# First loads in quarters, spread rows by DMA, and due-time ranks that reach into batch 1: a fused attention and MLP kernel

## The chip, the cores and the metric

The kernel runs on one core of a Trainium2 chip. The metric is the device time of one execution in microseconds. Beside the timed runs there is one execution recorded by the hardware profiler; every view quoted here is of such an execution. TensorE (PE in the rows, with PEld for its weight loads) multiplies matrices, VectorE (DVE), ScalarE (ACT) and GpSimd (POOL) do elementwise work, and SyncE (SP) issues most DMAs. Each engine runs its own instructions strictly in order.

## The reference, cut to what matters

```python
kv  = einsum('bhsd,bhse->bhde', k, v)            # 8 batches, 8 heads, 576 tokens, 64 wide
o   = einsum('bhsd,bhde->bhse', q, kv)
o   = o / sqrt(mean(o*o, -1) + 1e-6) * g_norm    # per head
x   = o as [batch, 576, 512]
tok = einsum('ts,bsd->btd', w_tok, alpha1*x + beta1)
u   = x + lam * tok
ch  = relu((alpha2*u + beta2) @ w_ch1) @ w_ch2   # 512 -> 2048 -> 512
out = u + lam * ch
```

All inputs and the output are f32. No softmax is involved, so K and V are multiplied first, into a 64 by 64 matrix for each head.

## The kernel before, in words

**Tiling.** A batch of 576 tokens is four chunks of 128 tokens and a tail of 64; the tails of two batches share a chunk, so that odd batches carry 640 columns through the channel products and even ones 512. For each batch TensorE computes: K times V (L674, tails L684; for batch 0 L610), q times that (L765 and L390; for batch 0 L772), token mixing (L854, tails L876; for batch 0 L906), the transposes of u (L941 in batches 0 and 1, by DMA later), 16 first channel products (ch1: L988 in even batches, L1002 in odd ones) and 16 or 20 groups of four second channel products (ch2: L1024). ScalarE applies ReLU to ch1's results (L979). VectorE normalises: squares on ScalarE (L800), then a sum (L802), a reciprocal (L808), the product with it (L821) and with alpha1, g and lam (L825, giving `rt`, the input of token mixing). GpSimd multiplies by g (L829).

**Startup.** Batch 0 is done in f32. `load_first` (L508) loads the four heads of a half of K and of V with one DMA each: 96 partitions, each with six consecutive tokens of 256 bytes per head (`six`, L463). `kv_first` (L599) multiplies them: six chunks of tokens times four heads, the heads in two column halves of TensorE, into one PSUM bank. `qt_first` (L624) turns q, its tail by four products with a 64 by 64 identity per half of the heads (L646). w_tok is transposed on TensorE (L1159, L1177). The weights w1 come in four loads, are cast by ScalarE and VectorE (L490, L491), and the products with beta2 give ch1's bias (L1255). w2 comes in four loads and is multiplied by lam (L1269) on VectorE or GpSimd. The rows lam, alpha2, e1 (alpha1 times g and lam) and g are needed on all 128 partitions: each is loaded as one row and spread by TensorE, a column of ones times the row (`spread`, L1089; product L1096), then copied from PSUM.

**Order of the work.** All operations go through `Prog.op` (L71) with an engine (or a choice of engines), a cost in us, and what they read and write. `schedule` (L169) is a list scheduler: it keeps a clock for every engine, gives each the first ready operation in order of priority (`pri`; the source order unless said otherwise) and so writes down the static order in which each engine will run. A DMA's end is modelled by one queue: `dma_free = max(dma_free, t + 0.3) + lat`, plus 2.0. Among TensorE's operations, only the first 16 in the order of priority are looked at once ch1 has begun; before that, a product of zeros (`warm`, L1330) fills in where nothing is ready. `hasten` (L105) walks back from targets with due times and gives everything that they depend on, SP's DMAs apart, a priority ahead of all else by the length of its way; `plan` (L122) then reschedules some rounds, computes each operation's latest start, ranks by it, and keeps the round whose modelled end is earliest. The targets were the 16 ch1 products of batch 0, 0.87 us apart (L1332). All else, batch 1's attention and token mixing among it, kept the source order; `merge` (L1296) sets that.

SP's loads are chained in their order (`P.chain`): the first K, V, q halves, w_tok, two loads of w1, batch 1's K and V, w1, batch 1's q, w1, then the four of w2, then batch 2.

Of the kernel before, what the change touches and what calls it, by code (L numbers as in the profile page):

```python
# [17 lines left out]
DM = 512  # L18
# [30 lines left out]
class Prog:  # L49
# [55 lines left out]
    def hasten(self, targets, step):  # L105

        rank, due = {}, {o: step * i for i, o in enumerate(targets)}
# [14 lines left out]
    def plan(self, targets, step, rounds):  # L122
# [3 lines left out]
        ahead = self.hasten(targets, step)  # L126
# [42 lines left out]
    def schedule(self):  # L169
# [226 lines left out]
def bass_transnormer_attn__then__resmlp_affine_kernel(  # L396
# [15 lines left out]
    with ExitStack() as stack:  # L412
# [50 lines left out]
        def six(tile, a):  # L463
            return tile[0:96, a].rearrange("p h c d -> p (h c d)")[:, 0:1536].rearrange(
                "p (h c d) -> p h c d", h=4, c=6)
# [27 lines left out]
        def load_main(tile, key, src, b, hs, eng="SP"):  # L493
# [4 lines left out]
                dma_us=3.6 * (hs.stop - hs.start) / 8)  # L498
# [9 lines left out]
        def load_first(a):  # L508
            for key, src, tile in (("kf", k, kf), ("vf", v, vf)):
                P.op("SP", 0.6, lambda e, src=src, tile=tile: e.dma_start(  # L510
                    six(tile, a).rearrange("p h c d -> p h (c d)"),
                    src[0, HALVES[a], :, :].rearrange("h (p c) d -> p h (c d)", c=6)),
                    w=[(key, a)], dma_us=2.05)

        def load_kv(b, go=()):
            j = (b + 1) % 2
            for tile, tl, src, n in ((kf, kft, k, "kf"), (vf, vft, v, "vf")):
# [3 lines left out]
                    r=go, w=[(n, j)], dma_us=3.6)  # L521
# [77 lines left out]
        def kv_first():  # L599

            def group(a):
                t = P.ptile(1)

                def f(e):
                    ks, vs = six(kf, a), six(vf, a)
                    for c in range(6):
                        for h in range(4):
                            o = t.flat(slice(64 * (h % 2), 64 * (h % 2) + 64))[
                                :, 64 * (h // 2):64 * (h // 2) + 64]
                            m = e.matmul(o, ks[:, h, c, :], vs[:, h, c, :],  # L610
                                         start=(c == 0 and h < 2), stop=(c == 5),
                                         skip_group_check=True)
                    return m
                P.op("PE", 1.7, f, r=[("kf", a), ("vf", a)], w=[t])
                for h in range(2):
# [3 lines left out]
                        t.flat(rows)[:, 0:128].rearrange("p (r e) -> p r e", r=2)),  # L619
                        r=[t, "kvz"], w=[("kv32", a, h)])  # L620
# [3 lines left out]
        def qt_first():  # L624

            def pair(pr):
# [9 lines left out]
                P.op("PE", 1.0, f, r=["ident", ("qf", pr // 2)], w=[t])  # L636
# [3 lines left out]
            def tail(a):  # L640
                t = P.ptile(1)

                def f(e):
                    for pr in range(2):
                        for h in range(2):
                            m = e.matmul(t.flat(slice(64 * h, 64 * h + 64))[  # L646
                                :, 64 * pr:64 * pr + 64], qft[0:64, 4 * a + 2 * pr + h, :],
                                ident[0:64, 0:64], start=True, stop=True)
                    return m
                P.op("PE", 0.4, f, r=["ident", "qft0"], w=[t])  # L650
# [326 lines left out]
        def ch1_groups(b):  # L977
            def relu(t, src, dst, fj, n):
                P.op("ACT", act_us(n) + 0.09, lambda e: e.activation(  # L979
                    dst, src(), ACT.Relu, bias=hb[:, fj:fj + 1]),  # L980
                    r=[t, ("hb", fj // 4)], w=[("ht", fj)])

            def even(fj):
# [9 lines left out]
                first_ch1.append(o)  # L993
                relu(t, lambda: t.flat(), ht[:, fj, 0:512], fj, 512)

            def odd(fj):
# [10 lines left out]
                P.op("PE", 1.1, f, r=[("w1", fj // 4)] + [("a2t", i) for i in range(5)],  # L1007
# [355 lines left out]
```

## Time and profile before

| | |
|---|---|
| median of 3 runs | 373.29 us (373.05 to 374.56) |
| the profiled execution | 372.88 us, its span 371.1 us |
| TensorE busy | 359.2 us, 97% of the span |
| VectorE, ScalarE, GpSimd busy | 197.0, 166.2, 79.9 us |
| DMA | 59.33 MB, mean 160 GB/s |
| granted TensorE clock | 0.999 |

The span runs from the first to the last instruction of the program. Busy time counts an instruction from its start to its modelled end; TensorE's products overlap one another, so a busy TensorE need not be at its peak. A row of the timeline reads: start, length, engine, line of the kernel, operation, out and in, shapes, count, and in brackets how long the engine idled before it and who ended that. In the chain of waits, each piece is a start, a length, and what the end of the program waited for at that time.

### The profile page before, as it was taken

How to read it: one execution, taken by the hardware profiler on the slowest of the kernel's cores; microseconds unless marked ns; L12 is line 12 of the kernel's file. 1: busy time of each engine (PE TensorE's matmuls, PEld its weight loads, DVE VectorE, ACT ScalarE, POOL GpSimd, SP SyncE). 2: the span in 40 equal slices, each digit the busy share in tenths (PEclk: the TensorE clock that was granted, in tenths of full speed). 3: DMA queues.
4: the chain of work that ended last, by engine and by line, in shares of the span. 5: the costliest groups of instructions: out<-in, count | busy, mean ns of one | idle time of the engine just before them, and what ended most of it. 6: DMA issues, size and time to landing. Idle time of an engine off the chain costs nothing.

```text
span 371.1 us, 6911 instructions
## 1 busy us (share of the span) xinstructions
PE 359.2 (97%) x3074; PEld 208.9 (56%) x2838; DVE 197.0 (53%) x300; ACT 166.2 (45%) x268; POOL 79.9 (22%) x69
## 2 busy tenths in 40 slices
PE   7999999999999999999999999999999999999995
PEld 3887665466654554457664554457654554457642
DVE  3267598976566467834836166924833175720021
ACT  1466797217862088206670087207730186007500
POOL 4046008520242005300242006200520006100000
PEclk9999999999999999999999999999999999999999
DMA  8999999989969399439923399423503110330021
GB/s 191 252 349 296 327 384 300 265 195 253 282 130 226 110 300 225 54 115 260 245 51 86 127 306 185 76 101 58 113 8 107 58 30 1 66 114 5 2 83 58
DMA packets 92456, 59.33 MB, mean 160 GB/s; under 512 B 59454, under 2 KB 83526, under 8 KB 92298
## 3 DMA queue, kind: packets, MB, share of 16 engines
q1 hardware_dynamic: 92400, 58.88, 63.1%
q8 instruction: 23, 0.38, 0.4%
q14 instruction: 7, 0.06, 0.0%
q10 hardware_dynamic: 26, 0.01, 0.0%
HBM read 38.04 MB, written 9.44 MB: 128 GB/s over the span
## 4 chain that ended last, share of the span: by engine, by line
PE 88%; DMA 4%; DVE 4%; ACT 1%; issue 1%; SPq 1%
PE ps L1024 30%; PE ps L1002 18%; PE ps L988 14%; PE ps L854 8%; PE ps L674 4%; DMA qf<-in_q_dram 4%; PE ps L390 2%; PE ps L765 2%; PE ps L876 1%; PE ps L906 1%; PE ps L941 1%; DVE small L802 1%; DVE rt L825 1%; PE ps L684 1%; SPq L510 1%
## 5 line engine op out<-in xcount | busy, mean ns | idle before, releaser
L1024 PE MATMUL ps<-w,ht 128*128 128x512 bf16 x551 | 126.0, 379 | 2.5 <-issue 1.7
L979 ACT ACTIVATE ht<-ps,hb 128x512 bf16<-128x512 f32 (+1 forms) x128 | 93.4, 742 | 46.0 <-PE ps L1002 38.8
L1024 PEld LDWEIGHTS ps<-w,ht 128*128 128x128 bf16 x576 | 54.5, 98 | 64.1 <-issue 1.2
L829 POOL TENSOR_TENSOR xm<-xm,g_bc 128x512 f32<-128x512 f32 (+1 forms) x36 | 46.4, 1288 | 190.3 <-DVE rt L825 188.4
L1002 PE MATMUL ps<-a2t,w 128*128 128x320 bf16 x512 | 72.0, 299 | 0.5 <-ACT ht L979 0.5
L1002 PEld LDWEIGHTS ps<-a2t,w 128*128 128x128 bf16 x512 | 49.2, 98 | 21.6 <-ACT ht L979 1.3
L988 PE MATMUL ps<-a2t,w 128*128 128x512 bf16 x246 | 57.0, 379 | 0.6 <-issue 0.2
L1033 DVE TENSOR_TENSOR xm<-ps,xm 128x512 f32<-128x512 f32 x32 | 22.1, 689 | 63.6 <-PE ps L1024 63.4
L701 ACT ACTIVATE kvd<-ps 64x128 bf16<-64x128 f32 x28 | 7.6, 272 | 86.0 <-PE ps L684 85.6
L988 PEld LDWEIGHTS ps<-a2t,w 128*128 128x128 bf16 x256 | 23.9, 98 | 26.3
L802 DVE TENSOR_REDUCE small<-sq 128x16 f32<-128x1024 f32 (+3 forms) x27 | 25.3, 936 | 23.6 <-ACT sq L800 23.6
L861 DVE TENSOR_TENSOR xm<-ps,xm 128x1024 f32<-128x1024 f32 x14 | 17.0, 1220 | 21.8 <-PE ps L854 21.8
L854 PE MATMUL ps<-rt,wt 128*128 128x512 bf16 x106 | 27.5, 379 | 0.4 <-DVE rtt L825 0.2
L800 ACT ACTIVATE sq<-ps 128x1024 f32<-128x1024 f32 (+3 forms) x27 | 21.6, 798 | 6.7 <-PE ps L772 3.5
L562 DVE TENSOR_TENSOR qs<-qf,qs 128x2048 bf16<-128x2048 f32 (+1 forms) x10 | 16.4, 1659 | 9.4 <-ACT qs L490 9.3
L706 DVE TENSOR_TENSOR kvd<-ps,kvd 64x128 bf16<-64x128 f32 x28 | 8.1, 289 | 25.0 <-ACT kvd L701 24.4
L765 PEld LDWEIGHTS ps<-kvd,qt 128*128 128x128 bf16 x280 | 17.9, 98 | 4.2
L821 DVE TENSOR_TENSOR xm<-ps,small 128x1024 f32<-128x1024 f32 (+1 forms) x18 | 19.7, 1098 | 0.4
L825 DVE TENSOR_TENSOR rt<-xm,e1g_bc 128x1024 bf16<-128x1024 f32 (+1 forms) x17 | 19.4, 1140 | 0.2
L490 ACT ACTIVATE qs<-qf 128x2048 bf16<-128x2048 f32 (+1 forms) x8 | 12.7, 1588 | 14.9 <-DMA qf<-in_q_dram 12.3
L390 PE MATMUL ps<-kvd,qt 128*128 128x64 bf16 x280 | 19.2, 193 | 0.0
L765 PE MATMUL ps<-kvd,qt 128*128 128x64 bf16 x280 | 19.1, 193 | 0.0
(107 smaller groups left out, 293.0 us busy)
## 6 DMA issues: line engine op xcount, KB each, us to landing
out_dram<-xm SPq DMA_DIRECT2D x32, 256.0 KB, 2.4
kf<-in_k_dram SPq DMA_DIRECT2D x7, 1024.0 KB, 9.5
vf<-in_v_dram SPq DMA_DIRECT2D x7, 1024.0 KB, 7.3
qf<-in_q_dram SPq DMA_DIRECT2D x7, 1024.0 KB, 8.7
stg<-in_moe_w_ch_dram SPq DMA_DIRECT2D x3, 1024.0 KB, 12.3
kf<-in_moe_w_ch_dram SPq DMA_DIRECT2D x2, 1024.0 KB, 14.5
kf<-in_k_dram SPq DMA_DIRECT2D x2, 576.0 KB, 8.4
vf<-in_v_dram SPq DMA_DIRECT2D x2, 576.0 KB, 10.4
```

The lines of the kernel that those rows point to most:

```text
L390: return pe.add_instruction(mybir.InstMatmult(start_tensor_calc=start, stop_tensor_calc=stop, tile_size=(128, 128), tile_position=(0, 0), ...
L765: e.matmul(o, w, kvd[:, h, 0, :], start=True, stop=False)
L800: P.op("ACT", act_us(64 * m), lambda e: e.activation(sqv, raw(), ACT.Square), r=[t], w=[("sq", sqs)])
L802: P.op("DVE", dve_us(64 * m), lambda e: e.tensor_reduce(out=smv, in_=sqv.rearrange("p (h d) -> p h d", h=m), axis=AX.X, op=ALU.add), r=[(" ...
L825: lambda e: e.tensor_tensor(out=r_, in0=x, in1=eb, op=ALU.mult),
L829: P.op("POOL", pool_us(64 * nh), lambda e, xc=xc: e.tensor_tensor(out=xc, in0=xc, in1=g_bc[rows, None, :].to_broadcast([nr, nh, DH]), op=A ...
L854: m = e.matmul(t.ap()[:, i, :], tok_w(b, sc, c), rsrc(b, sc), start=(sc == 0), stop=(sc == 4))
L979: P.op("ACT", act_us(n) + 0.09, lambda e: e.activation(dst, src(), ACT.Relu, bias=hb[:, fj:fj + 1]), r=[t, ("hb", fj // 4)], w=[("ht", fj)])
L988: m = e.matmul(t.flat(), w1[:, dj, 128 * fj:128 * fj + 128], a2t[:, dj, 0:512], start=(dj == 0), stop=(dj == 3))
L1002: m = e.matmul(t.ap()[:, i, 0:320], w1[:, dj, 128 * fj:128 * fj + 128], a2t[:, dj, 320 * i:320 * i + 320], start=(dj == 0), stop=(dj == 3))
L1024: m = e.matmul(t.flat(), ht[:, fj, 128 * c:128 * c + 128], w2[:, fj, :], start=(fj == 0), stop=(fj == 15))
L1033: P.op("DVE", dve_us(512), lambda e: e.tensor_tensor(out=x, in0=t.flat(), in1=x, op=ALU.add), r=[t] + keys, w=keys)
```

## The change

1. The first K and V: four DMAs of two heads take the place of two of four heads, per half. A pair of heads lies on 64 partitions, nine consecutive tokens (2,304 bytes) on each; the other pair on the other 64. `kv_first` multiplies nine chunks of tokens over 64 partitions, the heads alternating between the two halves of the rows, into two PSUM banks. New keys "kfg" and "vfg" stand for the second pair.
2. q's tail is turned by two transposes of two heads each, not by four products.
3. lam and alpha2 are no longer spread by TensorE; a DMA reads the row 128 times into all partitions (`spread_load`). lam's goes behind the last w1 load, alpha2's behind the last w2 load. The row load of alpha2 on ScalarE's queue goes; lam's row stays, for e1.
4. The planner: targets with due times are now ch1 of batch 0 (0.87 us apart), its ReLUs (each 1.5 steps behind its product), ch2 of batch 0 (from 16 us on, 0.87 apart) and the first ch1 product of batch 1 (36 us). All that these depend on, batch 1's attention and token mixing included, is ranked by due time, the targets too. Eight rounds are planned, not six.
5. The costs that the planner assumes for DMAs rise: q 4.2 us (3.6), K and V 3.8 (3.6), a start 0.6 us after issue (0.3); the quarters 1.05.

The diff, cut to its core:

```diff
-    def hasten(self, targets, step):
+    def hasten(self, due):
-        rank, due = {}, {o: step * i for i, o in enumerate(targets)}
+        rank = {}
...
-            if o not in due and o.eng != "SP":
+            if o.eng != "SP":
                 o.pri = -1000.0 - way
...
-        movable = [o for o in ahead if o.eng != "SP" and o not in targets]
+        movable = [o for o in ahead if o.eng != "SP"]
...
-            base = max(o.start - step * n for n, o in enumerate(targets))
-            for n, o in enumerate(targets):
-                late[o] = base + step * n
+            base = max(o.start - d for o, d in due.items())
+            for o, d in due.items():
+                late[o] = base + d
...
-                        dma_free = max(dma_free, t + 0.3) + pick.lat
+                        dma_free = max(dma_free, t + 0.6) + pick.lat
...
+        def nine(tile, a, g):
+            return tile[64 * g:64 * g + 64, a].rearrange("p h c d -> p (h c d)")[
+                :, 0:1152].rearrange("p (h c d) -> p h c d", h=2, c=9)
...
             for key, src, tile in (("kf", k, kf), ("vf", v, vf)):
-                P.op("SP", 0.6, lambda e, src=src, tile=tile: e.dma_start(
-                    six(tile, a).rearrange("p h c d -> p h (c d)"),
-                    src[0, HALVES[a], :, :].rearrange("h (p c) d -> p h (c d)", c=6)),
-                    w=[(key, a)], dma_us=2.05)
+                for g in range(2):
+                    P.op("SP", 0.45, lambda e, src=src, tile=tile, g=g: e.dma_start(
+                        nine(tile, a, g).rearrange("p h c d -> p h (c d)"),
+                        src[0, 4 * a + 2 * g:4 * a + 2 * g + 2].rearrange(
+                            "h (p c) d -> p h (c d)", c=9)),
+                        w=[(key, a)] if g == 0 else [(key + "g", a)], dma_us=1.05)
...
-                    r=go, w=[(n, j)], dma_us=3.6)
+                    r=go, w=[(n, j), (n + "g", j)], dma_us=3.8)
...
+                    for c in range(9):
+                        for h in (0, 2, 1, 3):
+                            g, r = h // 2, slice(64 * (h % 2), 64 * (h % 2) + 64)
+                            m = e.matmul(t.ap(r)[:, g, 0:64], nine(kf, a, g)[:, h % 2, c, :],
+                                         nine(vf, a, g)[:, h % 2, c, :],
+                                         start=(c == 0), stop=(c == 8), skip_group_check=True)
...
+                        h = 4 * a + 2 * pr
+                        m = e.transpose(t.flat()[:, 64 * pr:64 * pr + 64],
+                                        qft[0:64, h:h + 2, :].rearrange("p h d -> p (h d)"),
+                                        ident[0:64, 0:64])
...
+        def spread_load(src, dst, key):
+            P.op("SP", 0.6, lambda e: e.dma_start(dst[:], src[None, :].to_broadcast([128, DM])),
+                 w=[key], dma_us=0.9)
...
-        spread(("lam", "a2"))
...
-        first_ch1 = []
+        due = {}
+
+        def mark(b, ch, i, o):
+            if (b, ch) == (0, 0):
+                due[o] = 0.87 * i
+            elif (b, ch) == (0, 1):
+                due[o] = 16 + 0.87 * i
+            elif (b, ch, i) == (1, 0, 0):
+                due[o] = 36
...
         load_w(3)
+        spread_load(moe_lam, lam_bc, "lam")
...
             load_w(i)
+        spread_load(moe_alpha2, a2_bc, "a2")
...
-        P.plan(first_ch1[:16], 0.87, 6)
+        P.plan(due, 8)
```

More of the change, by code (lines that the diff above doesn't have):

```diff
@@ L644, in f @@
                     for pr in range(2):
[L645 to L648, printed above, removed]
+                        h = 4 * a + 2 * pr
+                        m = e.transpose(t.flat()[:, 64 * pr:64 * pr + 64],
+                                        qft[0:64, h:h + 2, :].rearrange("p h d -> p (h d)"),
+                                        ident[0:64, 0:64])
                     return m
-                P.op("PE", 0.4, f, r=["ident", "qft0"], w=[t])
+                P.op("PE", 0.28, f, r=["ident", "qft0"], w=[t])
                 P.op(act_dve(128), 0, lambda e: copy(
@@ L1026, in f @@
                     return m
[L1027 to L1028 removed]
+                o = P.op("PE", 0.87, f, r=[("w2", n)]
+                         + [("ht", i) for i in range(4 * n, 4 * n + 4)], w=[t])
+                mark(b, 1, 4 * n + c if b == 0 else 4 * c + n, o)
                 if n < 3:
@@ L1086, in load_params @@
                     r=["lamr", "e2r", "rtt0"], w=[("rtt1", i)])
-            spread(("e1", "g"))
-        def spread(names):
-            late = [] if "g" in names else [("wtm", sc) for sc in range(5)]
             for src, row, dst, key in params:
-                if key not in names:
+                if dst is None:
                     continue
```

62 lines of the change are left out of this document (25 added, 37 removed).

## The prediction

> **What bounds the kernel now.** I read the page's first line, then the busy time of each engine in four stretches: up to the first product of data, from there to the first channel product of batch 0, from there to the first channel product of batch 1, and the rest. Columns: stretch, its length, busy time of each engine, granted clock, share of the DMA engines, GB/s.
>
> ```profile
> span 371.1 us, 6911 instructions
> ...
> 0.00:9.00 9.00, 7.14 (x26) 2.75 (x26) 3.38 (x8) 1.49 (x2) 4.28 (x12) 1.00 0.82 187
> 9.00:42.36 33.36, 31.86 (x436) 26.41 (x440) 17.45 (x40) 19.42 (x41) 9.97 (x12) 1.00 1.09 302
> 42.36:86.11 43.75, 43.11 (x404) 24.63 (x371) 37.28 (x56) 25.65 (x48) 15.58 (x9) 1.00 1.03 285
> 86.11:371.10 284.99, 277.05 (x2213) 155.10 (x2004) 138.92 (x198) 119.61 (x179) 50.08 (x36) 1.00 0.52 123
> ```
>
> The reader is to see two things. TensorE (first figure) is busy almost without a break from 9.00 us on, at a clock of 1.00 throughout, so work taken off it can shorten the time. And up to 86.11 us the DMA engines are full as well (1.09, 1.03), after it half empty (0.52). The change acts ahead of 86.11 us; the last stretch I take as unchanged, apart from small shifts of a new plan.
>
> Busy time includes filler: products of zeros (L1330) that run where nothing else is ready. The same view for that line alone:
>
> ```profile
> 9.00:42.36 33.36, 2.07 (x8) 0.81 (x9) 1.00 1.09 302
> ```
>
> So of the 33.36 + 43.75 = 77.11 us between 9.00 and 86.11, TensorE spends 31.86 + 43.11 - 2.07 = 72.90 us on work, 2.07 on filler, and idles for 2.14. Filler and idle, 4.21 us, are all that a better order of this stretch could win; more must come from less work or an earlier start.
>
> Next the chain that ended last (start, length, what), to see what stands on TensorE's path:
>
> ```profile
> 32.69 1.05 PE ps L1096 x2
> ...
> 37.34 1.05 PE ps L1096 x2
> ...
> 58.86 1.03 ACT sq L800
> ...
> 72.87 1.90 PE ps L854 x8
> ```
>
> The two L1096 pairs spread lam and alpha2 over the partitions. From 58.86 to 72.87 the chain leaves TensorE: batch 1's attention output goes through ScalarE and VectorE before its token mixing (L854) may begin. Of TensorE's own waits, this one shows how the two runners meet there:
>
> ```profile
> PE ps L854 <- DVE rtt L825: 0.2, 1, 0.2
> ```
>
> TensorE, with second channel products of batch 0 as cover, and VectorE with batch 1 arrive within 0.2 us of each other.
>
> **The change part by part.** The sum is made against the profiled execution: 372.88 us, its span 371.1, hence 1.8 us outside the span; the median of the runs shown is 373.29, 0.41 above it.
>
> *Spreading lam and alpha2.* The change takes both pairs off TensorE and loads the rows already spread: 2 x 1.05 = **-2.10 us**, by the chain's rows above. Part of the second pair could otherwise have been a wait of the transposes around it for VectorE; I let it count, because batch 1's K and V products stand ready there as other work (they run at 39.83, below). ScalarE loses two copies and one small DMA issue, off the path. In exchange SP issues two DMAs of 256 KB; at the 336 GB/s of a row below that is 0.8 us of transfer each. The lam load goes ahead of the first w2 load, which SP issues at 37.20; lam's first user starts at 51.65, and what it makes is used from 61.32 on:
>
> ```profile
> 37.20 6.48 SPq L1263 DMA_DIRECT2D stg<-in_moe_w_ch_dram  x3
> ```
>
> ```profile
> 51.65 6.71 DVE L1269 TENSOR_TENSOR w<-stg,lam_bc 128x512 bf16<-128x512 f32 x11
> ```
>
> ```profile
> 61.32 11.39 PE L1024 MATMUL ps<-w,ht 128*128 128x512 bf16 x51
> ```
>
> The 9.7 us between the last two hide 0.8; without that cover it costs 0.8. The alpha2 load goes behind the last w2 load and ahead of batch 2's K and V, which TensorE multiplies after batch 1's token mixing, so after 72.87; alpha2's first user is batch 2's token mixing, in the last stretch. Nothing for either.
>
> *The first K and V in quarters.* What SP queues at the start, and what flows while the DMA engines are full (same columns as the first view):
>
> ```profile
> 0.73 0.40 SPq L510 DMA_DIRECT2D kf<-in_k_dram  x1
> 1.19 0.46 SPq L510 DMA_DIRECT2D vf<-in_v_dram  x1
> 1.70 0.48 SPq L494 DMA_DIRECT2D qf<-in_q_dram  x1
> ```
>
> ```profile
> 5.00:10.00 5.00, 5.00 (x53) 2.56 (x52) 2.77 (x4) 0.00 (x0) 0.33 (x2) 1.00 1.13 235
> ...
> 20.00:30.00 10.00, 9.79 (x89) 8.58 (x86) 7.28 (x17) 7.10 (x16) 4.35 (x5) 1.00 1.05 336
> ```
>
> ```profile
> kf<-in_k_dram SPq DMA_DIRECT2D x2, 576.0 KB, 8.4
> ```
>
> With equally full engines, the first stretch, mostly the first K and V (rows of 1,536 bytes over 96 partitions, by the code), flows at 235 GB/s, and the second (weights in rows of 2 KB, batch 1's K in rows of 1 KB, all over 128 partitions) at 336. The first halves of K and V are 2 x 576 KB = 1.18 MB: 5.0 us at the one rate, 3.5 at the other. Three things set the two apart: length of row, partitions, and the start itself. Quarters have rows of 2,304 bytes and in pairs cover 128 partitions, though each fills 64 only, which no row shows for a large load. So the first product starts 0 to 1.5 us earlier; I take **-1.0 us**, two of the three differences being gone. Of the four more DMAs (some 0.45 us of issue each), two stand ahead of the first part of q, hidden behind the 3.5 us of transfers queued in front; without that cover q comes 0.9 us later, beside the 1.05 us that spreading alpha1's row takes TensorE.
>
> A sentence apart: the Trainium skill's page "DMA: Bandwidth & Descriptors", section "Rules for kernel authors", advises against two transfers to disjoint halves of the partitions, as both go over the same 16 engines, and asks for one of 128 partitions; by it splitting brings nothing, which is a rival below.
>
> *K times V of batch 0.* Per group, 24 products over 96 partitions become 36 over 64; in f32 each is two instructions, so 48 become 72. The rows nearest to old and new form:
>
> ```profile
> 9.00 1.62 PE L610 MATMUL ps<-vf,kf 96*64 96x64 f32 x48
> 13.50 0.68 PE L646 MATMUL ps<-ident,qft 64*64 64x64 f32 x16
> ...
> 25.03 0.75 PE L1177 MATMUL ps<-ident,ht 64*128 64x64 f32 x5
> ...
> 39.83 1.98 PE L674 MATMUL ps<-vf,kf 128*64 128x64 f32 x62
> 41.74 0.46 PE L684 MATMUL ps<-vft,kft 64*64 64x64 f32 x16
> ```
>
> ```profile
> L684 PE MATMUL ps<-vft,kft x16: 218/218/267, 41.7 to 42.0; 64*64 64x64 f32 x16
> ```
>
> One instruction lasts some 0.22 us from start to end (the last row), so the step between starts is (0.46 - 0.22) / 15 = 16 ns in L684, which alternates between the halves of the rows as the new code does, (0.68 - 0.22) / 15 = 31 ns in L646, which stays in one half, and (1.98 - 0.22) / 61 = 29 ns in L674. New group by L684: 71 x 0.016 + 0.22 = 1.36 us against 1.62; by L646: 2.42. I take L684, whose order over the four tiles is the same: **-0.5 us** for both groups (at worst +1.6). The result takes two PSUM banks instead of one, at a time when hardly anything else wants a bank.
>
> *The tail of q.* 16 instructions at 31 ns, 0.5 us, become 4 transposes like L1177's, (0.75 - 0.22) / 4 = 0.13 us each: 0.5 us. Nothing.
>
> *New ranks, and the planner's costs of transfers.* Nothing is added on the chip; the instructions of each engine stand in another order. The worth lies between -4.21 us (all filler and idle gone) and a loss priced below; I take **0**: 4.21 us in 77 leave little to rank, and at 72.87 the two runners meet to 0.2 us already. load_kv's new keys add no wait: they name a product that it waits for anyway.
>
> Sum: -2.10 - 1.0 - 0.5 = -3.6. 372.88 - 3.6 = 369.28; with the 0.41 of the median, **369.7 us**. For this, batch 1's chain on VectorE must come some 3.6 us earlier too. It starts behind K and q products on TensorE and behind loads of the same queue, so I expect that it does.
>
> **The rivals.**
>
> (1) *VectorE takes the bound.*
>
> ```profile
> 61.32:72.87 11.55, 11.34 (x52) 4.97 (x52) 11.32 (x13) 5.18 (x9) 6.41 (x5) 1.00 1.13 266
> ```
>
> If batch 1's chain starts no earlier than now, L854 stays at 72.87, and a wait there takes the place of the work removed. TensorE then spends what it gained on the L1024 groups that now lie between later steps, like this one:
>
> ```profile
> 83.61 0.81 PE L1024 MATMUL ps<-w,ht 128*128 128x512 bf16 x3
> ```
>
> One such gap of 0.8 us may close: 373.29 - 0.8 = 372.5. For it: VectorE (third figure) is busy for 11.32 of 11.55 us. Against: ahead of 58.86 it scales w2 for 6.71 us (L1269), which isn't batch 1's and can be put behind.
>
> (2) *Ranking eats the cover; slower.* Batch 0's second channel products get due times from 16 us on, batch 1's attention products (L765, L390) only what follows from the 36 us of a far end. Each second-product group of four that goes ahead of them is 4 x 11.39 / 51 = 0.89 us less to run beside the 14.0 us from 58.86 to 72.87. Some 13 groups lie there now (11.39 / 0.89); three of the 16 are to spare. So it costs from the fourth on, and outweighs the 3.6 us gained from the eighth on. With ten ahead: 7 x 0.89 = 6.2 us, 375.9. For it: the due times as written. Against: these groups need scaled w2, from 51.65 on, no earlier than batch 1's first attention product runs now:
>
> ```profile
> 53.81 0.19 PE L765 MATMUL ps<-kvd,qt 128*128 128x64 bf16 x1
> ```
>
> (3) *The quarters load no faster*, because a half of the partitions holds back what longer rows give: 370.7. It is also what the page on DMA would give.
>
> (4) *The order wins too*: half of the 4.21 us goes, 367.6, if transfers planned nearer to their true times leave fewer waits for loads.
>
> **How the numbers follow.** Chances: forecast 0.42, (1) 0.20, (2) 0.22, (3) 0.07, (4) 0.09. A difference below 0.5% of 373.29, 1.9 us, is about what a measurement of this kernel can't tell from none. Faster by more (below 371.4): forecast, (3), (4): 0.58. Within: (1), 0.20. Slower (above 375.2): (2), 0.22. The range takes in (4), the ends of the start (-0.5 and +1.0) and of the tiles (+2.1) around 369.7, (1), and the nearer half of (2): 367.3 to 375.7. It leaves out the other half of (2) and the far end of (4). The forecast's own range is 368.7 to 371.4.
>
> **What would show it.** Right: L1096 only for alpha1 and g; a first product of K and V before 8.5 us, its 72 instructions in about 1.4 us; the first L1002 near 82.5 us and 285 us behind it. Wrong: L854 waits for VectorE by over a microsecond (rival 1; rival 2 if many L1024 run ahead of L765); the first product still at 9 us (rival 3); waits of L988 for w1, or more than 2 us of filler after the first product; a last stretch longer than 286 us, which I hold unchanged.

## The result, and the profile after

The changed kernel takes 375.77 us (median; 374.64 to 376.39) against 373.17 (372.24 to 374.56) for the kernel before on the same chip: a ratio of 1.0067, 95% interval 1.0053 to 1.0082. It is slower by 0.7%. The forecast was 369.7, faster by 1%, and the range ended at 375.7.

The same view by stretches as for the kernel before, cut at the first product of data, the first channel product of batch 0 and that of batch 1 (stretch, its length, busy time of TensorE, of its weight loads, of VectorE, ScalarE and GpSimd, granted clock, DMA share, GB/s):

```profile
0.00:10.43 10.43, 8.57 (x27) 3.21 (x27) 3.54 (x8) 1.49 (x2) 4.68 (x12) 1.00 0.83 191
10.43:42.07 31.64, 31.64 (x481) 25.52 (x481) 17.39 (x40) 16.22 (x35) 11.30 (x13) 1.00 1.07 313
42.07:87.87 45.80, 43.74 (x417) 24.39 (x371) 40.04 (x55) 24.84 (x45) 14.94 (x10) 1.00 0.91 277
87.87:373.88 286.01, 280.02 (x2246) 155.62 (x2006) 140.54 (x197) 119.45 (x182) 55.05 (x37) 1.00 0.52 123
```

The first channel product of batch 0 comes 0.3 us earlier than before (42.07 against 42.36), with 1.43 us lost ahead of the first product and 1.72 won behind it. The third stretch, 45.80 us, was 43.58 (in the timeline of before, batch 1's first L1002 starts at 85.94, a little ahead of the cut that I made there):

```profile
42.36:85.94 43.58, 42.94 (x402) 24.50 (x369) 37.15 (x55) 25.49 (x47) 15.58 (x9) 1.00 1.03 285
```

So 2.2 us are lost here. The last stretch is 0.9 longer. The sum, -0.3 + 2.2 + 0.9, is the 2.8 between the spans, 373.9 and 371.1.

The zeros' products alone, L1342 in the new numbering, in the second stretch:

```profile
10.43:42.07 31.64, 5.40 (x21) 1.71 (x20) 1.00 1.07 313
```

Filler grew from 2.07 to 5.40 us. Work on TensorE in this stretch fell from 31.86 - 2.07 = 29.79 to 31.64 - 5.40 = 26.24 us. So the work that the forecast took away is gone, and filler stands where it was. In the timeline of TensorE (start, length, instruction, count, idle time before it):

```profile
1.86 8.64 PE L1342 MATMUL ps<-a2b 128*128 128x512 bf16 x27 [1.86 <-DVE a2b L1127]
10.43 1.28 PE L610 MATMUL ps<-vf,kf 64*64 64x64 f32 x72
...
18.46 1.28 PE L610 MATMUL ps<-vf,kf 64*64 64x64 f32 x72
```

K times V is as fast as forecast: 72 instructions in 1.28 us, against 48 in 1.62. But the first stands behind 27 fillers (25 before), which the plan writes in ahead of it.

The chain that ended last now leaves TensorE earlier, ahead of the scaling of w2 (its longest pieces up to 80 us that bear on this):

```profile
1.86 8.64 PE ps L1342 x27
...
54.94 3.48 DVE w L1270 x4
59.55 6.02 DVE w L1270 x6
73.80 2.19 DVE rt L824
76.03 3.53 PE ps L853 x15
```

Token mixing of batch 1 starts at 76.03, before at 72.87. Ten scalings of w2 take VectorE 9.5 us here; in the kernel before eleven took 6.71. The view of that line alone says why (count; shortest, median and longest duration in ns; first and last start). The kernel before:

```profile
L1269 DVE TENSOR_TENSOR w<-stg,lam_bc x11: 684/685/693, 51.6 to 57.7; 128x512 bf16<-128x512 f32 x11
...
L1269 POOL TENSOR_TENSOR w<-stg,lam_bc x1: 3867/3867/3867, 55.6 to 55.6; 128x512 bf16<-128x512 f32 x1
```

The changed kernel:

```profile
L1270 DVE TENSOR_TENSOR w<-stg,lam_bc x10: 677/678/1760, 54.9 to 64.9; 128x512 bf16<-128x512 f32 x10
...
L1270 POOL TENSOR_TENSOR w<-kf,lam_bc x3: 1277/1602/1602, 58.6 to 61.6; 128x512 bf16<-128x512 f32 x3
```

Here the reader is to see two durations of one instruction. Alone, a scaling takes VectorE 0.68 us and GpSimd 1.27. Before, where GpSimd's ran into VectorE's eleven, GpSimd was held (3.87 us) and VectorE lost nothing. Now two of GpSimd's three take 1.60 and some of VectorE's 1.76.

TensorE's own waits behind the start (who waits for whom, us in all, times, longest):

```profile
PE ps L1002 <- ACT ht L978: 1.4, 1, 1.4
PE ps L1025 <- DVE xm L820: 1.2, 1, 1.2
PE ps L1002 <- ACT a2t L949: 0.6, 1, 0.6
PE ps L853 <- DVE rt L824: 0.3, 1, 0.3
```

The lower three belong to the third stretch; their 2.1 us are about what this stretch lost. The first, at 180 us in batch 3, is a ReLU that stands behind ScalarE's 1.90 us split of q (L490). In the kernel before, the one wait for a ReLU in the last stretch is 0.5 us.

### The profile page after: what moved, and what is told of

The parts are those of the page before. It is cut to its first block, busy times and chain, and to the rows that moved or that the text cites. A ratio compares the mean times of both kernels' runs of the same rounds, so it can differ in the third digit from the quotient of the medians.

```text
span 373.9 us, 7058 instructions
## 1 busy us (share of the span) xinstructions
PE 364.0 (97%) x3163; PEld 208.7 (56%) x2883; DVE 201.5 (54%) x300; ACT 162.0 (43%) x263; POOL 86.0 (23%) x72
## 4 chain that ended last, share of the span: by engine, by line
PE 90%; DVE 7%; ACT 2%; issue 1%
PE ps L1025 30%; PE ps L1002 18%; PE ps L988 13%; PE ps L853 8%; PE ps L673 4%; PE ps L1342 4%; DVE w L1270 3%; PE ps L764 2%; PE ps L390 2%; PE ps L875 1%; PE ps L771 1%; PE ps L905 1%; PE ps L631 1%; DVE rt L824 1%; DVE small L801 1%; ACT a2t L949 1%
## 5 line engine op out<-in xcount | busy, mean ns | idle before, releaser
L1025 PE MATMUL ps<-w,ht 128*128 128x512 bf16 x576 | 130.1, 379 | 1.2 <-DVE xm L820 1.2
L828 POOL TENSOR_TENSOR xm<-xm,g_bc 128x512 f32<-128x512 f32 (+1 forms) x36 | 49.7, 1380 | 196.0 <-DVE rt L824 194.1
L1002 PE MATMUL ps<-a2t,w 128*128 128x320 bf16 x512 | 72.2, 299 | 1.9 <-ACT ht L978 1.4
L1002 PEld LDWEIGHTS ps<-a2t,w 128*128 128x128 bf16 x512 | 49.3, 98 | 22.4 <-ACT ht L978 1.9
L988 PE MATMUL ps<-a2t,w 128*128 128x512 bf16 x256 | 58.2, 379 | 0.0
L853 PE MATMUL ps<-rt,wt 128*128 128x512 bf16 x112 | 28.8, 379 | 0.3 <-DVE rt L824 0.3
L564 DVE TENSOR_TENSOR qs<-qf,qs 128x2048 bf16<-128x2048 f32 (+1 forms) x10 | 17.2, 1738 | 2.6 <-ACT qs L490 2.5
L853 PEld LDWEIGHTS ps<-rt,wt 128*128 128x128 bf16 x112 | 10.8, 98 | 13.7 <-DVE rt L824 0.8
```

Source lines behind the costliest of these rows:

```text
L828: P.op("POOL", pool_us(64 * nh), lambda e, xc=xc: e.tensor_tensor(out=xc, in0=xc, in1=g_bc[rows, None, :].to_broadcast([nr, nh, DH]), op=A ...
L853: m = e.matmul(t.ap()[:, i, :], tok_w(b, sc, c), rsrc(b, sc), start=(sc == 0), stop=(sc == 4))
L988: m = e.matmul(t.flat(), w1[:, dj, 128 * fj:128 * fj + 128], a2t[:, dj, 0:512], start=(dj == 0), stop=(dj == 3))
L1002: m = e.matmul(t.ap()[:, i, 0:320], w1[:, dj, 128 * fj:128 * fj + 128], a2t[:, dj, 320 * i:320 * i + 320], start=(dj == 0), stop=(dj == 3))
L1025: m = e.matmul(t.flat(), ht[:, fj, 128 * c:128 * c + 128], w2[:, fj, :], start=(fj == 0), stop=(fj == 15))
```

## The experiments

All times are medians, with the ratio to the kernel before on the same chip and its 95% interval. Of an "edit" only the core is shown.

### One part undone, and the ranks alone

Three theories stood at the start: (1) the ranks hold up batch 1's normalisation; (2) the spread rows' DMAs hold up w2; (3) the quarters and the start cost time.

`old_rank`, the changed kernel with the old targets:

```diff
-        P.plan(due, 8)
+        P.plan(first_ch1[:16], 0.87, 6)
```

> The changed kernel with the old ranks (targets only the first channel products of batch 0, six rounds); loads in quarters, spread rows by DMA and the planner's DMA costs stay. Theory 1 (due times put the scaling of w2 into the middle of batch 1's normalisation on VectorE): token mixing of batch 1 begins at about 73 us instead of 76.03, and the time falls from 375.8 to 373 or below. Theory 2 (the DMAs that spread lam and alpha2 delay w2's loads by 3 us, and the scaling collides with the normalisation under any ranks): token mixing stays near 76 us and the time at 375 to 376. Theory 3 (the start with its quarters): little changes, 375 to 376.

Measured: 379.00 us, 1.0166 (1.0138 to 1.0194).

`old_loads`, the changed kernel with K and V in halves over 96 partitions:

```diff
-                for g in range(2):
-                    P.op("SP", 0.45, ... nine(tile, a, g) ..., dma_us=1.05)
+                P.op("SP", 0.6, ... six(tile, a) ..., dma_us=2.05)
```

> The changed kernel with the first K and V loaded and multiplied as before (halves over 96 partitions); all else as changed. Theory 3: the first product starts near 9 us instead of 10.43 and the time falls by 1 us or more, to 374.5 or below. Theories 1 and 2: the order on VectorE stays as changed, token mixing of batch 1 begins within 1 us of 76, and the time stays within 1 us of 375.8.

Measured: 378.51 us, 1.0137 (1.0112 to 1.0162).

`old_spread`, the changed kernel with lam and alpha2 spread by TensorE:

```diff
-        spread_load(moe_lam, lam_bc, "lam")
...
-        spread_load(moe_alpha2, a2_bc, "a2")
+        spread(("lam", "a2"))
```

> The changed kernel with lam and alpha2 spread by TensorE again; all else as changed. Theory 2: w2's first block lands near 49 us instead of 53, the scaling is over before the normalisation begins, and the time falls to 373.5 or below in spite of 2.1 us more products. Theory 1: the due times still cut the normalisation; 375.5 to 378.

Measured: 378.21 us, 1.0147 (1.0127 to 1.0167).

`rank_alone`, the kernel before with the new targets and eight rounds:

```diff
-        P.plan(first_ch1[:16], 0.87, 6)
+        P.plan(due, 8)
```

> The kernel before with the new ranks alone (due times up to batch 1's first channel product, eight rounds). Theory 1: the normalisation is cut here too, token mixing of batch 1 begins 2 us or more after 72.87, and the time is 375 to 376. Theories 2 and 3: w2 and the start are as before, so 372.5 to 374.

Measured: 372.21 us, 0.9998 (0.9971 to 1.0025). Seven of its ten executions lie between 371.6 and 372.8, three between 375.0 and 375.5.

No single part is the culprit: with any one of three taken out the kernel is slower still, and the ranks by themselves change nothing that can be measured. What the slow three share gave a fourth theory, (4): VectorE and GpSimd slow each other on the scaling of w2. In `old_rank`, in the timelines of VectorE, GpSimd and TensorE:

```profile
54.90 7.41 DVE L1270 TENSOR_TENSOR w<-stg,lam_bc 128x512 bf16<-128x512 f32 x5
...
53.73 8.02 POOL L1270 TENSOR_TENSOR w<-stg,lam_bc 128x512 bf16<-128x512 f32 x5 [18.25 <-DMA stg<-in_moe_w_ch_dram]
...
65.16 1.34 PE L988 MATMUL ps<-a2t,w 128*128 128x512 bf16 x4 [3.96 <-ACT ht L978]
```

Five scalings take VectorE 7.41 us, 1.48 each, beside GpSimd's five, and TensorE then idles for 3.96 us. In `rank_alone` the same work stands as in the kernel before: VectorE undisturbed, GpSimd held for 3.02 us.

```profile
L1272 DVE TENSOR_TENSOR w<-stg,lam_bc x11: 681/683/691, 53.5 to 59.8; 128x512 bf16<-128x512 f32 x11
...
L1272 POOL TENSOR_TENSOR w<-kf,lam_bc x4: 1270/1272/3022, 58.6 to 64.4; 128x512 bf16<-128x512 f32 x4
```

### The planner's costs

`costs_alone`, the kernel before with the new costs of DMAs and nothing else; `old_costs` is its opposite, the changed kernel with the old costs:

```diff
-                        dma_free = max(dma_free, t + 0.3) + pick.lat
+                        dma_free = max(dma_free, t + 0.6) + pick.lat
...
-                dma_us=3.6 * (hs.stop - hs.start) / 8)
+                dma_us=4.2 * (hs.stop - hs.start) / 8)
...
-                    r=go, w=[(n, j)], dma_us=3.6)
+                    r=go, w=[(n, j)], dma_us=3.8)
```

> The kernel before with the planner's new DMA costs alone (q 4.2, K and V 3.8, a start 0.6 us after issue). Nothing else differs, so only the order of the instructions can. Theory 4 (GpSimd and VectorE slow one another: planned later, five or six of the 16 scalings of w2 go to GpSimd while VectorE normalises batch 1 or scales w2 too, and each of these takes 1 to 1.6 us on VectorE instead of 0.6): first channel product of batch 1 at 88 us or later instead of 85.9, time 375.5 to 379. Theory 5 (costs are harmless, the loads or the spread rows are at fault): 372.5 to 374.

> The changed kernel with the old DMA costs of the planner for q, K, V and the start (the quarters keep 1.05). If the costs alone were at fault: 372 to 373.5. Theory 4 goes by what the plan does with w2: it still gives seven scalings to GpSimd beside batch 1's normalisation, so 374.5 to 377 and VectorE's scalings above 0.8 us on average. Theory 5: 375 to 376.5.

Measured: `costs_alone` 378.42 us, 1.0132 (1.0117 to 1.0148); `old_costs` 374.23, 1.0018 (0.9992 to 1.0044), its executions spread from 372.3 to 379.4. The second lies between the ranges that I had named and decides nothing. The first says that an edit that adds no work to the chip costs 5 us by itself. Its path, in the timelines of VectorE, ScalarE and TensorE of `costs_alone`:

```profile
53.98 5.81 DVE L1269 TENSOR_TENSOR w<-stg,lam_bc 128x512 bf16<-128x512 f32 x4
59.71 2.33 DVE L802 TENSOR_REDUCE small<-sq 128x16 f32<-128x1024 f32 x2
...
60.95 0.31 ACT L805 ACTIVATE small<-small,eps 128x16 f32<-128x16 f32 x1 [2.63 <-DVE small L802]
61.28 0.59 ACT L800 ACTIVATE sq<-ps 64x512 f32<-64x512 f32 x1
61.90 0.69 ACT L979 ACTIVATE ht<-ps,hb 128x512 bf16<-128x512 f32 x1
...
62.64 5.30 PE L988 MATMUL ps<-a2t,w 128*128 128x512 bf16 x12 [3.08 <-ACT ht L979]
```

Read it downwards. Four slowed scalings (1.45 us each) hold up the sum L802; ScalarE waits 2.63 us for that sum with its square root, and the ReLU (L979) behind the root in ScalarE's queue waits too, though its own product was long there; TensorE has no bank for its next channel product and idles for 3.08. Then its clock is halved (same columns as the first view; the third figure from the right is the granted clock):

```profile
61.60:68.40 6.80, 5.76 (x14) 2.09 (x15) 6.61 (x10) 4.51 (x9) 0.53 (x1) 0.50 1.04 248
```

The Trainium skill's page "TensorE: Matmul & The Clock Gate", section "Part 1: The HAM clock gate", says that the clock falls to half after an idle window of about 3.4 us. The trace agrees but for the size: the idle here was 3.08.

### Taking the contention away, with work left out

`small_pool`: the changed kernel, GpSimd writing zeros where it scaled w2. `costs_small_pool`: the same on `costs_alone`.

```diff
-  e.tensor_tensor(out=w2[:, 4 * n + hh, :], in0=s_[:, hh], in1=lam_bc[:], op=ALU.mult)
+  e.memset(w2[:, 4 * n + hh, :], 0.0) if e is nc.gpsimd else e.tensor_tensor(...)
```

> The changed kernel, same order on every engine; GpSimd's five scalings of w2 are replaced by writing zeros (so 5 of w2's 16 blocks are zero and the output is another). Theory 4: VectorE's ten scalings fall from 9.65 us to 6.5, token mixing of batch 1 begins at 74 us or before instead of 76.03, time 373.3 to 374.6. Theory 1 (the order on VectorE alone, w2 in the middle of the normalisation, is at fault): at most 0.5 us, 375.2 to 375.8.

> The kernel with the new transfer costs alone (378.4), same order on every engine, GpSimd's six scalings of w2 replaced by writing zeros, so six of the sixteen blocks of w2 are zero. By the theory of contention: VectorE's first four scalings fall from 1.45 to 0.61 us each, its other six to 0.61 as well, and of the 5 us lost against before most goes: 373.5 to 375, with no stretch of halved clock. By the theory that the order itself is bad (the normalisation stands behind late scalings on VectorE): 377 or more, the halved clock stays.

Measured: 373.70 us, 1.0004 (0.9994 to 1.0014), and 375.40, 1.0059 (1.0041 to 1.0078): 2.1 us less than the changed kernel, 3.0 less than `costs_alone` (0.4 above what I expected of it: VectorE's late scalings there still meet GpSimd's products with g). In `small_pool`, the line alone:

```profile
L1271 DVE TENSOR_TENSOR w<-stg,lam_bc x10: 681/684/686, 54.1 to 61.2; 128x512 bf16<-128x512 f32 x10
...
L1271 POOL MEMSET w<- x5: 524/524/655, 54.0 to 60.7; 128x512 bf16 x5
```

GpSimd is still busy in the same stretch, but only writes, and all ten of VectorE's last 0.68 us. So it is GpSimd's reading that holds VectorE, as far as this exchange shows it (a write of zeros is also shorter, 0.52 us). That is a rule of the Trainium skill, page "SBUF — State Buffer", section "Who interferes with whom": a VectorE instruction with two inputs in SBUF contends with a GpSimd one that reads SBUF, not with one that only writes. The trace agrees (1.76 against 0.68 us). The section also calls the shared ports an exclusive lock and lets the order of issue decide who blocks. GpSimd's 3.87 and 3.02 us above agree with that; `after_unbroken` below does not. I did not weigh the rule in the prediction.

### Fillers ahead of the first product; all scaling on VectorE

`fewer_fill`: the last 9 of the 27 fillers ahead of the first product left out. `after_dve`: all of w2's scaling on VectorE.

```diff
+        drop(9, False)        # fewer_fill: takes fillers out of the finished plan
```

```diff
-                    P.op(dve_pool(512), 0, lambda e, hh=hh: e.tensor_tensor(
+                    P.op("DVE", dve_sb(512), lambda e, hh=hh: e.tensor_tensor(
```

> The changed kernel, same order; the last 9 of the 27 products of zeros ahead of the first product are left out. If these hold the first product back: it starts at 8.7 to 9.0 us, when v's last quarter has landed (8.68), instead of 10.43. If the first channel product then comes earlier by as much, the time falls by 1 to 1.7 us; if it waits for q, w_tok and VectorE anyway, as the equal 42 us of all variants so far suggest, by less than 0.7.

> The changed kernel with all sixteen scalings of w2 on VectorE and planned so; nothing left out. By the theory of contention: each 0.61 us, 9.8 us of VectorE in place of 10.3 us in the changed kernel, so that the stage is a little shorter only, 374.5 to 375.5: taking GpSimd's work onto the engine that bounds the stage gives away what the contention cost. By the rival that any GpSimd work beside VectorE is the whole loss: 373.0 to 373.7.

Measured: 375.38 us, 1.0051 (1.0036 to 1.0066), and 375.28, 1.0054 (1.0036 to 1.0073). The second went as expected: sixteen undisturbed scalings (0.69 us each) take VectorE as long as ten held ones. The first went by the smaller of its two cases: the first product comes 1.4 us earlier, the first channel product 0.6 (41.49) and the end 0.4. From it also comes the answer on the quarters, in TensorE's timeline:

```profile
1.86 5.84 PE L1342 MATMUL ps<-a2b 128*128 128x512 bf16 x18 [1.86 <-DVE a2b L1127]
9.05 1.28 PE L610 MATMUL ps<-vf,kf 64*64 64x64 f32 x72 [1.35 <-DMA vf<-in_v_dram]
```

Nothing stands ahead of the product but the last quarter of V, and it starts at 9.05 us; in the kernel before at 9.00. One execution says little here, but the landing of V says the same in all that were profiled. The first half, issued at 1.2 us, lands 7.3 to 7.8 us later, at 8.5 to 9.0 (seven executions). The second of the two quarters that take its place, issued at 2.9, lands 5.6 to 6.9 us later, at 8.5 to 9.8 (thirteen).

### The other two parts alone

`spread_alone` and `quarters_alone`: the kernel before with part 3, and with part 1 of the change.

```diff
-        spread(("lam", "a2"))                 # spread_alone
+        spread_load(moe_lam, lam_bc, "lam")
...
+        spread_load(moe_alpha2, a2_bc, "a2")
```

```diff
-                P.op("SP", 0.6, ... six(tile, a) ..., dma_us=2.05)      # quarters_alone
+                for g in range(2):
+                    P.op("SP", 0.45, ... nine(tile, a, g) ..., dma_us=1.05)
```

> The kernel before with lam and alpha2 spread by DMA alone; loads, ranks and planner costs as before. Its plan puts 6 scalings of w2 on GpSimd beside VectorE's stretch of normalisation, and 4 of VectorE's late. By the theory of contention: VectorE's scalings over 1.0 us each where GpSimd's run beside them, the stretch from the first channel product of batch 0 to the first of batch 1 some 46 to 50 us and the time 375 to 379; the 2.1 us of TensorE work saved shows as later fillers. By the prediction's sum: 373.2 less 2.1 = 371.1.

> The kernel before with the quarters and the new K·V group alone (their planner costs come with them); ranks and spreading as before. Its plan puts 5 of the 16 scalings of w2 on GpSimd, all but one of them behind VectorE's ten. By the theory that the loss is VectorE and GpSimd slowing each other on w2: if GpSimd's five stand behind VectorE's ten and do not overlap, VectorE's scalings stay at 0.61 us each and the time is that of before, 373; if they overlap, 1.0 us or more each and 376 to 378. By the theory of the prediction (each part adds its own saving): 373.2 less 1.5 = 371.7. By the theory that the quarters themselves cost: 376 or more with VectorE's scalings at 0.61 us each.

Measured: `spread_alone` 373.04 us, 0.9989 (0.9977 to 1.0002); `quarters_alone` 377.94, 1.0114 (1.0077 to 1.0151), spread from 374.8 to 379.6. For the first I expected a loss, and none came, although GpSimd scales seven blocks there and VectorE is held. VectorE's timeline shows why:

```profile
65.00 2.35 DVE L825 TENSOR_TENSOR rt<-xm,e1g_bc 128x1024 bf16<-128x1024 f32 x2
67.39 1.65 DVE L825 TENSOR_TENSOR rtt<-xtl,e1g_bc 64x512 bf16<-64x512 f32 x1
69.06 6.67 DVE L1268 TENSOR_TENSOR w<-kf,lam_bc 128x512 bf16<-128x512 f32 x4
```

Four of the slowed scalings, 1.67 us each, stand behind batch 1's normalisation (`rt`, `rtt`), not ahead of it. So slowed work cost little where nothing on the path was queued behind it. With this, theory (2) falls: the rows spread by DMA cost nothing by themselves. They gain nothing either, against the prediction's 2.1 us: behind the first product, TensorE's order has 14 fillers here and 7 in the kernel before.

### Only a wait added: GpSimd behind VectorE

If holding VectorE is the loss, it must go when GpSimd's last scalings wait for VectorE's run; each engine's order stays, nothing is left out. The plan's times have it so anyway: it treats the two engines as excluding each other on w2, but tells the chip nothing of it.

```diff
+        for o in first:               # GpSimd's scalings planned behind VectorE's run
+            o.deps.add(run_[-1])      # ... wait for the last of that run
```

`after_held`, `costs_held` and `quarters_held` are the changed kernel, `costs_alone` and `quarters_alone` with it.

> The changed kernel, the same order on every engine, nothing left out; GpSimd's last four scalings of w2 also wait for the last of VectorE's ten, as the plan's times have them anyway. By the theory that one of the two engines keeps the other from reading while it reads, so that it matters who comes first: all ten of VectorE's scalings last 0.68 us (in the changed kernel some last 1.76), the stage from the first channel product of batch 0 to that of batch 1 shrinks from 45.8 to 43.6 us and the time is 373.3 to 374.3. By the rival that the changed order itself costs the time, or that a wait more on GpSimd holds up second channel products instead: 375.8 or more.

> The kernel with the new transfer costs alone (378.4), same order, nothing left out; four or five of GpSimd's scalings also wait for VectorE's first run of four. By the theory of who comes first: those four fall from 1.45 to 0.68 us each, the wait of 3.1 us for ReLU goes and with it the stretch of halved clock, 373.5 to 375.5. By the rival that the order costs the time: 378.

> The kernel with the quarters alone (377.9), same order, nothing left out; GpSimd's last five scalings also wait for VectorE's ten. By the theory of who comes first: VectorE's ten fall from 0.93 to 0.68 us each, 2.5 us of VectorE's path, and the time is 372.5 to 374.5: the quarters by themselves then neither gain nor cost. By the theory that the quarters cost something of their own: 376 or more with VectorE's ten at 0.68 us.

Measured: 373.61 us, 1.0008 (0.9999 to 1.0016), from 375.77; 374.97, 1.0047 (1.0034 to 1.0059), from 378.42; 373.65, 1.0027 (1.0008 to 1.0045), from 377.94. A wait makes all three kernels faster, by 2.2, 3.5 and 4.3 us. `costs_held` is still 0.5% slower than the kernel before; what makes up that rest was not tried. VectorE's and GpSimd's scalings in `after_held`:

```profile
58.44 3.69 DVE L1270 TENSOR_TENSOR w<-stg,lam_bc 128x512 bf16<-128x512 f32 x6
...
62.21 1.28 POOL L1270 TENSOR_TENSOR w<-stg,lam_bc 128x512 bf16<-128x512 f32 x1 [7.17 <-DVE w L1270]
63.57 3.96 POOL L1270 TENSOR_TENSOR w<-kf,lam_bc 128x512 bf16<-128x512 f32 x3
```

The six that took 6.09 us in the changed kernel take 3.69, and GpSimd's, later, are no longer slowed either (1.3 us each).

### Who comes first

`after_unbroken`: VectorE's first sum of batch 1 moved behind all ten scalings, so that VectorE is already in an unbroken run when GpSimd's blocks arrive.

```diff
+        for o in rest:                # the six scalings behind the sum ...
+            P.sequence.remove(o)
+        at = P.sequence.index(brk)    # ... go ahead of it
+        P.sequence[at:at] = rest
```

> The changed kernel with one instruction moved: VectorE's first sum of squares of batch 1 stands behind all ten scalings of w2 and not between the fourth and the fifth, so that VectorE is in an unbroken run when GpSimd's blocks arrive; nothing left out, no wait added. By the theory of who comes first: all ten last 0.68 us, the first of GpSimd's three is held for 2 us or more (over 3 us long, as it was 3.87 in the kernel before), and the time is 373.3 to 374.5. By the rival that both engines slow each other whoever comes first: VectorE's scalings stay at 1.0 us in the mean, 375.8 or more.

Measured: 378.83 us, 1.0152 (1.0139 to 1.0166). The theory of who comes first falls, and its rival stands:

```profile
53.80 11.48 DVE L1270 TENSOR_TENSOR w<-stg,lam_bc 128x512 bf16<-128x512 f32 x10
...
59.29 4.84 POOL L1270 TENSOR_TENSOR w<-kf,lam_bc 128x512 bf16<-128x512 f32 x3 [1.40 <-DMA kf<-in_moe_w_ch_dram]
```

GpSimd's three come into VectorE's run at 59.29 and are not held as in the kernel before; the two engines alternate, and ten scalings take 11.48 us. What decides between "GpSimd is held" and "they alternate" stays open; coming second does not.

### Without the fillers

`no_later_fill`: the changed kernel without those 9 fillers ahead of the first product and without the 20 behind it. `held_no_fill`: the same on `after_held`.

```diff
+        drop(9, True)
```

> The changed kernel without the last 9 of the 27 fillers ahead of the first product and without the 20 fillers behind it (products of zeros that nothing uses); order otherwise the same. By the theory that the TensorE work saved ahead of the first channel product only turned into filler, because other engines and loads set when that product can start: TensorE's own waits take the fillers' place, named by VectorE, GpSimd or loads, the first channel product stays between 41.3 and 42.5 us and the time between 375 and 376. By the rival that the fillers themselves hold up the start: the first channel product at 39 to 40 us, 372 to 373.

> The changed kernel in which GpSimd's last scalings also wait for VectorE's ten, without the 9 late fillers ahead of the first product and the 20 behind it; the order otherwise the same, no work of the reference left out. By the theory both losses are apart: 373.6 less 0 to 0.5, so 373.1 to 373.6, no different from the kernel before. By the rival that the fillers hold up the start: 370 to 371.

Measured: 373.19 us, 0.9987 (0.9965 to 1.0009), and **371.29, 0.9949 (0.9927 to 0.9971)**. Here I was wrong again: I took the fillers to cover waits that would be there anyway. In `no_later_fill` the first channel product comes at 40.88 us. In `held_no_fill`, TensorE's timeline:

```profile
8.80 1.28 PE L610 MATMUL ps<-vf,kf 64*64 64x64 f32 x72
...
21.35 2.05 PE L771 MATMUL ps<-kvd,qt 128*128 128x128 f32 x16 [0.27 <-ACT qt L490]
...
35.55 1.09 PE L940 MATMUL ps<-ident,xm 128*128 128x128 f32 x8 [0.94 <-DVE xm L922]
...
39.20 2.97 PE L988 MATMUL ps<-a2t,w 128*128 128x512 bf16 x13 [0.16 <-issue]
```

The first channel product comes at 39.20, 2.9 us ahead of the changed kernel's and 3.2 ahead of the kernel before's. Where the 20 fillers stood (4.3 us at 0.22 from one start to the next), TensorE now idles for 2.2 us in all (it is busy for 28.24 of the 30.40 us from 8.80 to 39.20), 0.94 at most at once. The fillers were too many: the plan writes them in for waits that it models, and on the chip they run whether the data are there or not. With both losses out, the change is the fastest version measured, 0.5% ahead of the kernel before. The kernel before has fillers too (25 and 7) and was not run without them, so it is not shown how much of this lead is the change's own.

In `no_later_fill` the fillers are seen to have had a use as well, though that the wait is the cause was not tried: 2.5 us after a wait of 2.09 us for V, ahead of the first product, TensorE's transposes of q ran at half speed. Its timeline:

```profile
9.84 1.28 PE L610 MATMUL ps<-vf,kf 64*64 64x64 f32 x72 [2.09 <-DMA vf<-in_v_dram]
...
12.33 3.63 PE L631 MATMUL ps<-ident,qf 128*64 128x128 f32 x32
```

They took 1.97 us in the kernel before. The stretch in question, in the columns of the first view:

```profile
12.40:15.90 3.50, 3.50 (x33) 3.17 (x33) 0.00 (x0) 1.20 (x2) 0.00 (x0) 0.51 1.04 221
```

The granted clock is 0.51.

## Why the prediction was wrong

Two steps failed, by about as much each. Of the 6.1 us between 375.77 and the forecast's 369.7, VectorE and GpSimd meeting on w2 makes 2.2 (375.77 to 373.61, `after_held`), surplus filler 2.3 (373.61 to 371.29, `held_no_fill`) and the last stretch 0.9. The quarters' missing gain of 1.0 would be enough for the other 0.7; this rest was not taken apart.

*The first step that failed* is "New ranks, and the planner's costs of transfers", which I took at 0 because nothing is added on the chip and only the order changes. The costs alone, without ranks, are worth +5 us (`costs_alone`), the ranks alone nothing that can be measured. I bounded the loss by the cover that ranking eats, rival (2). That did not come: batch 0's second channel products start at 60.79, behind batch 1's first attention product at 54.85. The order did something else: it put GpSimd's reading of w2 beside VectorE's, ahead of batch 1's normalisation. In the changed kernel this costs 375.77 - 373.61 = 2.2 us, shown by one added wait.

*The second: spreading, -2.10, and K times V, -0.5.* The work went, 3.55 us of it in the second stretch, K times V in 1.28 us as worked out. That work taken off TensorE shortens the time was my reason, since it was "busy almost without a break". It failed because the plan put filler where work was taken away: filler grew by 3.3 us, to 5.40, and more than 2 us of it was one of the signs that I had named. `spread_alone`, with the first term alone, gains nothing measurable (0.9989) and has twice the fillers. Without the surplus fillers the step comes nearly true: first L1002 at 82.83 in `held_no_fill` (I had said near 82.5), 286.0 us behind it (I had said 285).

*The quarters, -1.0.* Rival (3) was right that they load no faster: 9.05 us against 9.00 with nothing but V ahead, and V lands at 8.5 to 9.8 us against 8.5 to 9.0. Why, no run shows. The result agrees with the section of the Trainium skill's page "DMA: Bandwidth & Descriptors" that the prediction cites.

*Rival (1), VectorE takes the bound,* came true in direction: L853 starts 3.2 us later, 76.03 against 72.87, and the chain runs through VectorE. Its mechanism was only half of it. I had priced a chain that starts no earlier, not one whose instructions get longer, so that my 372.5 had the wrong sign. The forecast needed batch 1's chain on VectorE 3.6 us earlier; I had said that I expected so and checked only what it stands behind, not what runs beside it. The row was there: GpSimd's one scaling of 3.87 us beside 1.28 for its like, in a profile that I had read.

*The last stretch* I held unchanged; it is 0.9 us longer, by a ReLU of batch 3 behind a split of q (a wait of 1.4 us; before, 0.5). `after_held` and `held_no_fill` have it too.

*What stays open:* why VectorE keeps its pace in the kernel before and in `rank_alone`, and not in the others; and the spread of `old_costs` and `quarters_alone` over 5 to 7 us. That an execution can fall either way between the two patterns would explain the spread, but no run shows it, and three of the eleven executions of `quarters_held`, where GpSimd waits, still lie at 375.6 to 375.9 us.

## What to carry to other kernels

A change of a planner's costs is a change of the kernel: list which of VectorE's products of two SBUF inputs come to stand beside GpSimd instructions that read SBUF, and give both the longer durations, ahead of whatever is queued behind. Where a plan assumes that two engines exclude each other, make the chip keep to it; one wait was worth 2 to 4 us here. Before counting work taken off a busy engine as time, see whether filler is written into its order, and run once without it.

## What the runs showed of the hardware that I had not expected

- VectorE's product of two SBUF inputs (128x512, f32 in, bf16 out) takes 0.68 us alone and 1.76 when it meets GpSimd's; GpSimd's takes 1.27 alone, 1.60 in alternation, and 3.02 and 3.87 where it was shut out. Against GpSimd's zeros VectorE loses nothing.
- After TensorE idled for 3.08 us in `costs_alone` the granted clock was 0.50 in a stretch of 6.8 us. TensorE was busy for 5.76 of it, at half speed; by an estimate from that, 2.9 us more are lost, so the idle time is paid about twice. A wait of 2.09 us near the start (`no_later_fill`) and one of 2.21 in `old_loads` were followed by such stretches too; one of 2.1 us in `old_spread` and those of 1.2 to 1.4 us in the changed kernel were not.
